# Global keys between the blocks of K^T, a tile of its own for the normalised P, and given steps for the weight conversion

## The chip, the cores and the metric

The kernel runs on one core of a Trainium2 chip. The metric is the device time of one execution in microseconds (us), as the median of several executions. The profile that is read here is of one such execution.

## What is computed

Windowed attention with a few global tokens, and behind it two feed-forward networks, all in fp32:

```
q_l, k_l, v_l: 4 batches x 8 heads x 512 local tokens x 64;   q_g, k_g, v_g: 4 x 8 x 32 global tokens x 64
out_g = softmax(q_g @ [k_g, k_l]^T / 8) @ [v_g, v_l]
s_ll  = q_l @ k_l^T / 8, masked to |i - j| <= 32
out_l = softmax([q_l @ k_g^T / 8, s_ll]) @ [v_g, v_l]
x = concat(out_g, out_l) as 2176 tokens x 512
h = x @ w_in   (512 x 2048);  x = (h * cos(h)) @ w_out   (2048 x 512)
h = x @ w2_in  (512 x 2048);  out = max(h, 0)^2 @ w2_out
```

The weights arrive as float64. The kernel reads them as pairs of 32-bit words and makes an fp32 number of each pair (the conversion), and then splits every fp32 weight and activation into a high and a low part for products in TensorE's fp32r form.

## The kernel before

**Attention.** There are 16 pairs of heads (4 batches x 4). A pair gives two local items of 256 query tokens each, and two pairs share one global item, so that an order of five items repeats eight times: local, local, local, local, global; 40 items in all. One step of the main loop (`for s in range(...)`) takes one item each through several stages, at fixed lags: item s has its scores made on TensorE (PE), item s gets its softmax on VectorE (DVE) and ScalarE (ACT), item s-1 is normalised on GpSimd (POOL) and DVE, item s-2 has its probabilities transposed on PE, item s-3 has those transposes copied out by ACT, item s-4 is multiplied by V. The order of the stages within a step is the list `CFG["order"]`, and every engine works through its own instructions in that order: nothing overtakes.

The names that the rows use: `tk` and `tq` are PE's transposes of K and Q in PSUM, `kT` and `qT` their copies in SBUF; `s` the local scores and `sg` the global ones; `pt` the local probabilities, `pg` their normalised part for the global keys; `st` row sums and their reciprocals; `tw`, `tg` transposes of probabilities and `tws`, `tgs` their copies (`twg`, `tlg`, `ptg`, `tls` for the global item); `o` the output of an item, `xt` its place in the networks' input. `kn`, `qn`, `va`, `vb`, `qgn`, `ktn`, `vgz` are loads.

**K^T.** `kT` of a pair holds 8 rows of 160 columns: 64 keys, the next 64 keys, 32 global keys, so that the scores of one 64-token query block read one row. ACT writes the first 64 columns of each row (`k_evac`, line 336); POOL copies the next row's first 64 columns beside them (line 351), repeats the global keys in all rows (line 353) and puts the tail of the sequence into the last row (line 361). The normalising step (`norm`, lines 468 and 475) works in place in `pt`: one of four units on DVE, three on POOL.

**The conversion of weights.** `Feed` takes jobs (weight block g, half q) one by one. `begin` starts a job when its credit has reached 1 and issues its load `raw` on SyncE's queue (SP, lines 126 and 131); two calls later POOL and ACT make `cu` and `cc` (lines 143 and 146), one call later DVE combines them (lines 154 and 155), and one call later POOL adds them into the ring tile `r` (line 165). In attention `begin` is called once a step and gets 0.5 of credit from step 5 on, except in the steps whose number modulo 5 is 0 or 2 while pairs are left; in the networks it gets 0.5 in every step. `split` makes `w` of a finished block: ACT writes the high parts (line 228, twice), and at the next call of `split` POOL and DVE subtract them (line 214). In attention it is called in the steps of `CFG["split"]`.

The items' number modulo 5 also says what else a step holds: K^T of a later pair in steps 2 and 4 (modulo 5), Q^T in steps 0 and 3, loads of Q and copies of V in step 1, of V in step 3, of K in step 0.

**PSUM and queues.** The transposes `tk`, `tq`, `tw`, `twg` take turns in two banks, `s` and `sg` in three. All loads but Q's first are issued by SP, in program order, on eight semaphores in turn: a load waits for the landing of the one eight places before it.

**Networks.** 160 steps of 24 matmuls each (`g1` into `h`, `g2` into `y`), on the blocks of weights that `split` left; their first four steps are interleaved with attention's last.

Of the kernel before, what the change touches and what calls it, by code (L numbers as in the profile page):

```python
# [10 lines left out]
F32 = mybir.dt.float32  # L11
# [3 lines left out]
AF = mybir.ActivationFunctionType  # L15
ALU = mybir.AluOpType
# [3 lines left out]
P = 128  # L20
NEG = -8.0e9
# [4 lines left out]
CFG = {'order': ['CV', 'LQ', 'S', 'TE', 'BG', 'LK', 'OM', 'TRK', 'KEV', 'CC', 'SM',  # L26
           'RC', 'NM', 'CB', 'LV', 'OE', 'TRQ', 'QE', 'KC', 'TM'],
 'lag': {'S': 0,
         'TRK': -3,
         'TRQ': -2,  # L30
         'KEV': -3,
         'KC': -3,
         'QE': -2,
         'SM': 0,
# [9 lines left out]
         'CV': 11},  # L44
 'ndv': 1,
 'teg': 'AA',
 'free': -5,
 'kb': 'P',
 'split': [22, 24, 27, 29, 33],
 'sx': [32, 34, 37, 39],  # L50
 'arate': 0.5,
 'rate': 0.5,
 's0': 5,
 'groups': [[4, 5, 7], [8, 8]],
 'xd': [0, 1, 2, 3],
 'nr': 6,
 'oe': 'DD',
 'sgb': 0}
GROUPS = CFG["groups"]
RATE, ARATE, XD, NRING = CFG["rate"], CFG["arate"], CFG["xd"], CFG["nr"]  # L60

@with_exitstack
def kernel(
# [14 lines left out]
    nc = tc.nc  # L78
    B, H, SL, D = q_l.shape
    SG = q_g.shape[2]  # L80
# [26 lines left out]
    ident = cpool.tile([P, P], F32, name="ident")  # L107
# [123 lines left out]
    feed = Feed()  # L231
# [21 lines left out]
    lp = late.enter_context(tc.tile_pool(name="lp", bufs=1, side="right"))  # L253
    ep = early.enter_context(tc.tile_pool(name="ep", bufs=1))

    KTB = 2 * 64 + SG
    masks = [ep.tile([P, 160], F32, name=f"mask{i}") for i in range(3)]
    VA = [lp.tile([P, 5, 4, D], F32, name=f"va{i}") for i in range(2)]
    VB = [lp.tile([P, 4, 4, D], F32, name=f"vb{i}") for i in range(2)]
# [2 lines left out]
    ktail = ep.tile([P, NPAIR, B, 64], F32, name="ktail")  # L262
# [3 lines left out]
    kn, qn, kT, qT, tks = {}, {}, {}, {}, {}  # L266
# [54 lines left out]
    def tr_k(p):  # L321
        b, kk = divmod(p, NPAIR)
        tk = bank(BT, "tk")
        for c in range(4):
            nc.tensor.transpose(  # L325
                tk[:, c * P : (c + 1) * P],
                kn[p // 2][:, c, 2 * (p % 2) : 2 * (p % 2) + 2].rearrange("p h d -> p (h d)"),
                ident,
            )
        t = ep.tile([P, 8, KTB], F32, tag="kT", name="kT", bufs=3)  # L330
        kT[p] = t
        tks[p] = tk

    def k_evac(p):
        t, tk = kT[p], tks.pop(p)
        nc.scalar.activation(
            t[:, :, 0:64], tk.rearrange("p (j q) -> p j q", q=64), AF.Copy
        )
        if CFG["kb"] == "A":
            nc.scalar.activation(  # L340
                t[:, :, 128:KTB], tk[:, 0:SG].unsqueeze(1).to_broadcast([P, 8, SG]), AF.Copy
            )
        elif CFG["kb"] == "D":
            nc.vector.tensor_copy(
                t[:, :, 128:KTB], tk[:, 0:SG].unsqueeze(1).to_broadcast([P, 8, SG])
            )

    def k_copy(p):
        t = kT[p]
        one = dict(scalar1=1.0, scalar2=1.0, op0=ALU.mult, op1=ALU.mult)  # L350
        nc.gpsimd.tensor_scalar(t[:, 0:7, 64:128], t[:, 1:8, 0:64], **one)
        if CFG["kb"] == "P":
            nc.gpsimd.tensor_scalar(
                t[:, :, 128:KTB], t[:, 0, 0:SG].unsqueeze(1).to_broadcast([P, 8, SG]), **one
            )
        if p > 1:
            k_tail(p)

    def k_tail(p):
        b, kk = divmod(p, NPAIR)  # L360
        nc.gpsimd.tensor_scalar(
            kT[p][:, 7, 64:128], ktail[:, kk, b, :], 1.0, 1.0, op0=ALU.mult, op1=ALU.mult
        )

    def tr_q(p):
# [37 lines left out]
        load_small(qgn, q_g[b], b)  # L403

    class Local:
# [4 lines left out]
        def s_mm(self):  # L413
            self.s = [bank(BS, "s") for h in range(2)]
            for i in range(2):
                for half in range(2):
                    j = 4 * self.hb + 2 * i + half
                    for h in range(2):
                        d = slice(64 * h, 64 * h + 64)
                        nc.tensor.matmul(  # L420
                            self.s[h][64 * half : 64 * half + 64, 160 * i : 160 * i + 160],
                            lhsT=qT[self.p][d, 64 * j : 64 * j + 64],
                            rhs=kT[self.p][d, j, :],
                            start=True,
                            stop=True,
                            skip_group_check=True,
                        )

        def softmax(self):
            self.pt = lp.tile([P, 4, KTB], F32, tag="pt", name="pt", bufs=4)  # L430
            self.st = lp.tile([P, 3, 4], F32, tag="st", name="st", bufs=4)

            def unit(u):
                i = 2 * self.hb + u % 2
                m = masks[1] if i == 0 else masks[2] if i == 3 else masks[0]
                nc.vector.tensor_tensor_reduce(  # L436
                    out=self.pt[:, u, :],
                    in0=self.s[u // 2][:, 160 * (u % 2) : 160 * (u % 2) + 160],
                    in1=m,
                    scale=-0.125,  # L440
                    scalar=3.0e38,
                    op0=ALU.add,
                    op1=ALU.min,
                    accum_out=self.st[:, 0, u : u + 1],
                )
                nc.scalar.activation(  # L446
                    self.pt[:, u, :],
                    self.pt[:, u, :],
                    AF.Exp,
                    bias=self.st[:, 0, u : u + 1],  # L450
                    scale=-1.0,
                    accum_out=self.st[:, 1, u : u + 1],
                )

            return [lambda u=u: unit(u) for u in range(4)]
# [10 lines left out]
        def norm(self):  # L466
            self.pg = lp.tile([P, 4, SG], F32, tag="pg", name="pg", bufs=2)
            nc.gpsimd.tensor_tensor(
                self.pg,
                self.pt[:, :, P:KTB],  # L470
                self.st[:, 2, :].unsqueeze(2).to_broadcast([P, 4, SG]),
                op=ALU.mult,
            )
            for u in range(4):
                (nc.vector if u < CFG["ndv"] else nc.gpsimd).tensor_scalar(
                    self.pt[:, u, 0:P],
                    self.pt[:, u, 0:P],
                    self.st[:, 2, u : u + 1],
                    1.0,
                    op0=ALU.mult,  # L480
                    op1=ALU.mult,
                )

        def t_mm(self):
            self.tw = bank(BT, "tw").rearrange("p (u q) -> p u q", u=4)
            self.tg = bank(BG, "tg")[:, 0:P]
            for u in range(4):
                nc.tensor.transpose(self.tw[:, u, :], self.pt[:, u, 0:P], ident)  # L488
            nc.tensor.transpose(self.tg, self.pg.rearrange("p u q -> p (u q)"), ident)

        def t_evac(self):
# [42 lines left out]
    class Global:  # L534
# [3 lines left out]
        def s_mm(self):  # L538
            self.s = []
            for n in (320, 256):  # L540
                s = bank(BT if CFG["sgb"] >> (n == 256) & 1 else BS, "sg")
                self.s.append(s)
                for i in range(2):
                    kk = 2 * self.g + i
                    t = kT[self.b * NPAIR + kk]
                    nc.tensor.matmul(  # L546
                        s[64 * i : 64 * i + 64, 0:n],
                        lhsT=qgbd[:, kk, self.b, :],
                        rhs=t[:, 0:5, 0:64] if n == 320 else t[:, 5:8:2, 0:128],
                        start=True,  # L550
                        stop=True,
                    )
# [96 lines left out]
    for h in range(2):  # L649
        s = slice(64 * h, 64 * h + 64)  # L650
        nc.gpsimd.affine_select(
            out=masks[0][s, 0:64], in_=masks[0][s, 0:64], pattern=[[1, 64]],
            compare_op=ALU.is_ge, fill=NEG, base=0, channel_multiplier=-1,
        )
        nc.gpsimd.affine_select(
            out=masks[0][s, 64:128], in_=masks[0][s, 64:128], pattern=[[-1, 64]],
            compare_op=ALU.is_ge, fill=NEG, base=0, channel_multiplier=1,
        )
    for i in (1, 2):
        nc.vector.tensor_copy(masks[i], masks[0])  # L660
    nc.vector.memset(masks[1][0:64, 0:32], NEG)
    nc.vector.memset(masks[2][64:128, 96:128], NEG)
    nc.vector.memset(qgbd, 0.0)

    nc.gpsimd.memset(ktail, 0.0)
# [7 lines left out]
    for b in range(B):  # L673
        for g in range(2):
            for i in range(2):
                p = b * NPAIR + 2 * g + i
# [227 lines left out]
    for s in range(L["TRK"], NI + L["OE"]):  # L904
        due = lambda k: due_tr.get(s - k)
        cb, qe = [], []
        for c in CFG["order"]:
            if c == "BG":
                cb = feed.begin(ARATE if due(CFG["free"]) is None else 0.0) if s >= CFG["s0"] else []
            elif c == "CB":  # L910
                for op in cb:
                    op()
# [111 lines left out]
```

## Time and profile before

| | us |
|---|---|
| median of 3 runs | 911.26 (911.12 to 912.29) |
| the profiled execution's own time | 911.74 |
| its span (first to last instruction) | 910.0 |
| PE busy | 890.7 (98%) |
| DVE, ACT, POOL busy | 502.5, 439.4, 447.8 |

PE's busy time is a sum over instructions whose ends are modelled, so that 98% does not say that PE is at its peak. Attention takes the first 146 us, the networks the rest.

### The profile page before, as it was taken

How to read it: one execution, taken by the hardware profiler on the slowest of the kernel's cores; microseconds unless marked ns; L12 is line 12 of the kernel's file. 1: busy time of each engine (PE TensorE's matmuls, PEld its weight loads, DVE VectorE, ACT ScalarE, POOL GpSimd, SP SyncE). 2: the span in 40 equal slices, each digit the busy share in tenths (PEclk: the TensorE clock that was granted, in tenths of full speed). 3: DMA queues.
4: the chain of work that ended last, by engine and by line, in shares of the span. 5: the costliest groups of instructions: out<-in, count | busy, mean ns of one | idle time of the engine just before them, and what ended most of it. 6: DMA issues, size and time to landing. Idle time of an engine off the chain costs nothing.

```text
span 910.0 us, 15436 instructions
## 1 busy us (share of the span) xinstructions
PE 890.7 (98%) x5720; PEld 793.7 (87%) x5720; DVE 502.5 (55%) x1058; ACT 439.4 (48%) x1036; POOL 447.8 (49%) x517
## 2 busy tenths in 40 slices
PE   7899999999999999999999999999999999999997
PEld 5777777999999999999999988889999888899996
DVE  5687899866776666765554483433422833232221
ACT  5778787665655545545444553333334632222211
POOL 4577888754574435744342484444423842222221
PEclk9999999999999999999999999999999999999999
DMA  7888643221122111121110021111100101010001
GB/s 168 192 192 195 165 129 94 71 70 53 49 62 70 47 53 61 50 70 47 47 47 1 1 70 47 53 44 66 47 1 1 47 1 47 1 47 1 35 35 36
DMA packets 82075, 57.10 MB, mean 63 GB/s; under 512 B 58320, under 2 KB 74704, under 8 KB 82000
## 3 DMA queue, kind: packets, MB, share of 16 engines
q1 hardware_dynamic: 79824, 55.59, 22.0%
q8 instruction: 45, 0.74, 0.3%
q10 hardware_dynamic: 2176, 0.52, 0.3%
q14 instruction: 30, 0.25, 0.1%
HBM read 47.45 MB, written 4.46 MB: 57 GB/s over the span
## 4 chain that ended last, share of the span: by engine, by line
PE 91%; DVE 3%; DMA 2%; ACT 1%; SPq 1%; POOL 1%; issue 1%; ACTq 0%; POOLq 0%; DVEq 0%
PE h L757 41%; PE y L786 41%; PE s L420 2%; PE tw L488 1%; PE o L504 1%; PE tq L368 1%; DVE pt L436 1%; PE o L516 1%; PE og L622 1%; DMA raw<-in_moe_w_out_dram 1%; PE sg L546 1%; PE tk L325 0%; ACT pt L446 0%; SPq L292 0%; PE twg L603 0%
## 5 line engine op out<-in xcount | busy, mean ns | idle before, releaser
L757 PE MATMUL h<-x,w 128*128 128x436 f32 (+3 forms) x1920 | 403.4, 358 | 0.0
L857 POOL TENSOR_TENSOR glo<-cr,ghi 128x436 fp32r<-128x436 f32 (+3 forms) x160 | 186.8, 1167 | 407.7 <-ACT ghi L851 393.9
L757 PEld LDWEIGHTS h<-x,w 128*128 128x128 f32 x1920 | 354.6, 188 | 27.5
L786 PE MATMUL y<-ghi,w 128*128 128x436 f32 (+1 forms) x640 | 177.6, 358 | 0.0
L846 DVE TENSOR_TENSOR cr<-h,cr 128x436 f32<-128x436 f32 (+3 forms) x160 | 96.6, 605 | 134.0 <-ACT cr L837 115.0
L786 PE MATMUL y<-w,ghi 128*128 128x512 f32 x544 | 168.4, 390 | 0.0
L745 DVE TENSOR_TENSOR x<-xt,x 128x436 fp32r<-128x436 f32 (+3 forms) x100 | 102.5, 1035 | 93.3 <-ACT x L744 78.3
L837 ACT ACTIVATE cr<-h 128x384 f32<-128x384 f32 (+1 forms) x80 | 42.8, 535 | 210.7 <-PE h L757 209.4
L786 PEld LDWEIGHTS y<-ghi,w 128*128 128x128 f32 x640 | 120.3, 188 | 6.1
L786 PEld LDWEIGHTS y<-w,ghi 128*128 128x128 f32 x544 | 101.4, 188 | 18.9
L786 PE MATMUL y<-glo,w 128*128 128x436 f32 (+1 forms) x320 | 114.8, 359 | 0.0
L786 PE MATMUL y<-w,glo 128*128 128x512 f32 x272 | 106.8, 393 | 0.0
L851 ACT ACTIVATE ghi<-cr 128x436 fp32r<-128x436 f32 (+3 forms) x160 | 89.7, 560 | 24.5 <-DVE cr L846 23.6
L831 ACT ACTIVATE ck<-h 128x436 int32<-128x436 f32 (+1 forms) x80 | 42.6, 532 | 113.1 <-PE h L757 113.1
L833 DVE SCALAR_TENSOR_TENSOR cr<-h,ck 128x436 f32<-128x436 f32 (+1 forms) x80 | 48.6, 607 | 84.9 <-ACT ck L831 84.9
L165 POOL TENSOR_TENSOR r<-cu,cc 128x512 uint32<-128x512 uint32 x64 | 85.0, 1328 | 2.0 <-DVE cc L155 2.0
L744 ACT ACTIVATE x<-xt 128x436 fp32r<-128x436 f32 (+3 forms) x100 | 55.1, 560 | 20.2 <-PE h L757 19.9
L786 PEld LDWEIGHTS y<-glo,w 128*128 128x128 f32 x320 | 60.1, 188 | 2.7
L786 PEld LDWEIGHTS y<-w,glo 128*128 128x128 f32 x272 | 51.0, 188 | 10.8
L842 ACT ACTIVATE cr<-cr,halfpi 128x436 f32<-128x436 f32 (+1 forms) x80 | 52.5, 657 | 10.1 <-DVE cr L833 10.1
L155 DVE SCALAR_TENSOR_TENSOR cc<-raw,cc 128x512 uint32<-128x512 uint32 x64 | 55.7, 870 | 0.0
L446 ACT ACTIVATE pt<-pt,st 128x160 f32<-128x160 f32 x128 | 53.3, 425 | 4.1 <-DVE st L436 4.1
(91 smaller groups left out, 907.4 us busy)
## 6 DMA issues: line engine op xcount, KB each, us to landing
raw<-in_moe_w_in_dram SPq DMA_DIRECT2D x32, 512.0 KB, 3.7
raw<-in_moe_w_out_dram SPq DMA_DIRECT2D x32, 512.0 KB, 3.5
vb<-va SPq DMA_DIRECT2D x16, 256.0 KB, 4.6
out_dram<-ypart SPq DMA_DIRECT2D x16, 256.0 KB, 2.1
qn<-in_q_l_dram SPq DMA_DIRECT2D x28, 128.0 KB, 3.7
va<-in_v_l_dram SPq DMA_DIRECT2D x24, 128.0 KB, 3.3
kn<-in_k_l_dram SPq DMA_DIRECT2D x21, 128.0 KB, 3.0
va<-in_v_l_dram SPq DMA_DIRECT2D x8, 96.0 KB, 3.2
```

The costliest lines, as they stand in the source:

```text
L155: lambda: v.scalar_tensor_tensor(c, t[:, :, 1].bitcast(U32), 0x80000000, c, op0=ALU.bitwise_and, op1=ALU.bitwise_or,),
L165: nc.gpsimd.tensor_tensor(ring[g][:, q, :].bitcast(U32), u, c, op=ALU.add)
L446: nc.scalar.activation(self.pt[:, u, :], self.pt[:, u, :], AF.Exp, bias=self.st[:, 0, u : u + 1], scale=-1.0, accum_out=self.st[:, 1, u : ...
L744: nc.scalar.activation(hi, xr, AF.Copy)
L745: return lambda: (nc.vector if kk in XD else nc.gpsimd).tensor_tensor(lo, xr, hi.bitcast(F32), op=ALU.subtract)
L757: nc.tensor.matmul(h, lhsT=w[:, ws, 0, kk * P : (kk + 1) * P], rhs=x, start=(k == 0), stop=(k == 3 * NK - 1),)
L786: nc.tensor.matmul(o, lhsT=l, rhs=r, start=(c_first and k == 0), stop=(c_last and k == 2))
L833: lambda: nc.vector.scalar_tensor_tensor(r, h, INV2PI, k, op0=ALU.mult, op1=ALU.subtract),
L842: nc.scalar.activation(ctmp[s], ctmp[s], AF.Sin, bias=halfpi, scale=TWOPI)
L846: nc.vector.tensor_tensor(r, hps.pop(s), r, op=ALU.mult)
L851: nc.scalar.activation(ghi[s], ctmp[s], AF.Copy)
L857: nc.gpsimd.tensor_tensor(lo, ctmp.pop(s), hi.bitcast(F32), op=ALU.subtract)
```

## The change

Four things. (1) `kT` has 9 rows of 96 columns: 64 keys and the 32 global keys behind them. The scores of block j read 160 columns from 96j on, which are block j, the global keys and block j+1. So line 351 is gone, and the masks and slices follow the new order of columns. (2) `norm` writes the normalised local part into a tile `pn` (2 buffers) instead of into `pt`, whose buffers go from 4 to 3. (3) Conversion in attention begins in 13 listed steps, and `split` is called in other steps. (4) In the networks the credit is 0.55 a step. Only the last two move instructions between steps.

```diff
- 'free': -5,
- 'split': [22, 24, 27, 29, 33],
+ 'split': [21, 26, 31, 36, 39],
- 'arate': 0.5,
- 'rate': 0.5,
- 's0': 5,
+ 'begin': [9, 11, 14, 16, 19, 21, 24, 26, 29, 31, 34, 36, 39],
+ 'rate': 0.55,
...
+    GK = slice(64, 64 + SG)
...
-        t = ep.tile([P, 8, KTB], F32, tag="kT", name="kT", bufs=3)
+        t = ep.tile([P, 9, 64 + SG], F32, tag="kT", name="kT", bufs=3)
...
     def k_copy(p):
-        nc.gpsimd.tensor_scalar(t[:, 0:7, 64:128], t[:, 1:8, 0:64], **one)
-        if CFG["kb"] == "P":
-            nc.gpsimd.tensor_scalar(
-                t[:, :, 128:KTB], t[:, 0, 0:SG].unsqueeze(1).to_broadcast([P, 8, SG]), **one
-            )
+        nc.gpsimd.tensor_scalar(
+            t[:, 0:8, GK], t[:, 0, 0:SG].unsqueeze(1).to_broadcast([P, 8, SG]), **one
+        )
...
+    def windows(t, u):
+        return t.rearrange("p u q -> p (u q)")[:, KTB * u : KTB * u + 192].rearrange(
+            "p (a q) -> p a q", a=2
+        )[:, :, 0:64]
...
-                            rhs=kT[self.p][d, j, :],
+                            rhs=kT[self.p].rearrange("p j q -> p (j q)")[d, 96 * j : 96 * j + KTB],
...
-            self.pt = lp.tile([P, 4, KTB], F32, tag="pt", name="pt", bufs=4)
+            self.pt = lp.tile([P, 5, KTB], F32, tag="pt", name="pt", bufs=3)
...
-                self.pt[:, :, P:KTB],
+                self.pt[:, 0:4, GK],
...
+            self.pn = lp.tile([P, 4, P], F32, tag="pn", name="pn", bufs=2)
             for u in range(4):
                 (nc.vector if u < CFG["ndv"] else nc.gpsimd).tensor_scalar(
-                    self.pt[:, u, 0:P],
-                    self.pt[:, u, 0:P],
+                    self.pn[:, u].rearrange("p (a q) -> p a q", a=2),
+                    windows(self.pt, u),
...
-                nc.tensor.transpose(self.tw[:, u, :], self.pt[:, u, 0:P], ident)
+                nc.tensor.transpose(self.tw[:, u, :], self.pn[:, u], ident)
...
-                cb = feed.begin(ARATE if due(CFG["free"]) is None else 0.0) if s >= CFG["s0"] else []
+                cb = feed.begin(1.0 if s in CFG["begin"] else 0.0)
```

The changed kernel's lines stand two to five lower in number: its 124, 129, 141, 144, 163, 212, 226 are before's 126, 131, 143, 146, 165, 214, 228, and its 342, 463, 471 are 353, 468, 475.

On SP's queue, around step 16 (the load of Q in `qn`), before:

```order
L309 DMA vb_88<-va_86 64x1024
L310 DMA vb_88<-va_86 64x1024
L292 DMA qn<-in_q_l_dram 128x4x64 x4
L397 DMA qgn<-in_q_g_dram 32x8x64
L131 DMA raw<-in_moe_w_out_dram 128x1024
L299 DMA va_85<-in_v_g_dram 32x4x64
```

and changed:

```order
L308 DMA vb_88<-va_86 64x1024
L309 DMA vb_88<-va_86 64x1024
L291 DMA qn<-in_q_l_dram 128x4x64 x4
L129 DMA raw<-in_moe_w_out_dram 128x1024
L386 DMA qgn<-in_q_g_dram 32x8x64
L298 DMA va_85<-in_v_g_dram 32x4x64
```

The weight load of step 18 is now that of step 16, and its two readers stand in step 18 instead of step 20.

On POOL, from the end of step 15 to step 18, before (`ptg` closes step 15, `cu` opens step 16, and the K^T copies close step 17):

```order
L595 TENSOR_SCALAR ptg<-ptg,stg 128x544
L143 TENSOR_SCALAR cu<-raw 128x512
L468 TENSOR_TENSOR pg<-pt,st 128x128
L475 TENSOR_SCALAR pt<-pt,st 128x128 x3
L468 TENSOR_TENSOR pg<-pt,st 128x128
L475 TENSOR_SCALAR pt<-pt,st 128x128 x3
L351 TENSOR_SCALAR kT<-kT 128x7x64
L353 TENSOR_SCALAR kT<-kT 128x8x32
L361 TENSOR_SCALAR kT<-ktail 128x64
L165 TENSOR_TENSOR r<-cu,cc 128x512
L468 TENSOR_TENSOR pg<-pt,st 128x128
L475 TENSOR_SCALAR pt<-pt,st 128x128 x3
```

and changed:

```order
L591 TENSOR_SCALAR ptg<-ptg,stg 128x544
L141 TENSOR_SCALAR cu<-raw 128x512
L463 TENSOR_TENSOR pg<-pt,st 128x128
L471 TENSOR_SCALAR pn<-pt,st 128x128 x3
L463 TENSOR_TENSOR pg<-pt,st 128x128
L471 TENSOR_SCALAR pn<-pt,st 128x128 x3
L342 TENSOR_SCALAR kT<-kT 128x8x32
L350 TENSOR_SCALAR kT<-ktail 128x64
L141 TENSOR_SCALAR cu<-raw 128x512
L163 TENSOR_TENSOR r<-cu,cc 128x512
L463 TENSOR_TENSOR pg<-pt,st 128x128
L471 TENSOR_SCALAR pn<-pt,st 128x128 x3
```

The big copy of K^T is gone, and step 18 has a `cu`, which waits for a weight load, ahead of its `r` and its normalising.

On ACT, steps 21 to 23, before (`tws<-twg` belongs to step 22, the `kT` behind it too):

```order
L446 ACTIVATE pt,st<-pt,st 128x160 x4
L611 ACTIVATE tws<-twg 128x512
L612 ACTIVATE tls<-tlg 32x128
L336 ACTIVATE kT<-tk 128x8x64
L446 ACTIVATE pt,st<-pt,st 128x160 x4
L228 ACTIVATE w<-r 128x512 x2
L494 ACTIVATE tws<-tw 128x512
```

and changed:

```order
L441 ACTIVATE pt,st<-pt,st 128x160 x4
L226 ACTIVATE w<-r 128x512 x2
L607 ACTIVATE tws<-twg 128x512
L608 ACTIVATE tls<-tlg 32x128
L335 ACTIVATE kT<-tk 128x8x64
L441 ACTIVATE pt,st<-pt,st 128x160 x4
L490 ACTIVATE tws<-tw 128x512
```

The two writes of `w` have gone from the end of step 22 to the end of step 21.

## Rows read from the trace of the kernel before

**Rows 1.** The page's first part: busy us (share) xinstructions.

```profile
PE 890.7 (98%) x5720; PEld 793.7 (87%) x5720; DVE 502.5 (55%) x1058; ACT 439.4 (48%) x1036; POOL 447.8 (49%) x517
```

**Rows 2.** Stretches: length, busy us of PE, PEld, DVE, ACT, POOL, clock, DMA.

```profile
50.00:100.00 50.00, 47.49 (x730) 38.06 (x726) 41.07 (x188) 39.57 (x148) 38.93 (x78) 0.97 0.82 187
100.00:150.00 50.00, 46.93 (x717) 36.85 (x716) 43.67 (x173) 39.97 (x146) 42.68 (x77) 1.00 0.47 125
200.00:250.00 50.00, 50.00 (x257) 48.03 (x256) 33.51 (x49) 29.73 (x58) 25.92 (x23) 1.00 0.18 55
```

**Rows 3.** Line 351's instructions: duration ns min/median/max, first and last start us.

```profile
L351 POOL TENSOR_SCALAR kT<-kT x16: 556/561/986, 6.5 to 130.4; 128x448 f32<-128x448 f32 x16
```

**Rows 4.** PE in order of time: start, us, operation [idle before <-releaser].

```profile
99.64 0.66 PE L603 MATMUL twg<-ident,ptg 128*128 128x128 f32 x4 [0.45 <-POOL ptg L595]
109.74 1.03 PE L488 MATMUL tw<-ident,pt 128*128 128x128 f32 x3 [0.25 <-POOL pt L475]
```

**Rows 5.** POOL in order of time, ahead of the first of these.

```profile
96.39 1.26 POOL L214 TENSOR_TENSOR w<-r,w 128x512 fp32r<-128x512 f32 x1
```

**Rows 6.** Step 23 on ACT and PE, in order of time.

```profile
85.81 1.14 ACT L228 ACTIVATE w<-r 128x512 fp32r<-128x512 f32 x2
87.49 0.98 PE L368 MATMUL tq<-ident,qn 128*128 128x128 f32 x4 [0.61 <-ACT tws L494]
```

**Rows 7.** The stretch behind it; the clock stands after the busy times.

```profile
86.00:92.00 6.00, 5.39 (x58) 4.05 (x57) 4.00 (x17) 4.45 (x15) 3.65 (x10) 0.72 0.57 128
```

**Rows 8.** DVE and PE around steps 33 to 35, in order of time.

```profile
124.81 0.68 DVE L214 TENSOR_TENSOR w<-r,w 128x512 fp32r<-128x512 f32 x1
...
128.20 0.77 PE L420 MATMUL s<-kT,qT 64*64 64x160 f32 x14 [1.30 <-ACT ptg L571]
```

**Rows 9.** PE in the first steps of the networks.

```profile
151.00 0.28 PE L606 MATMUL tlg<-ident,ptg 128*32 128x128 f32 x1 [0.68 <-ACT tgs L498]
```

**Rows 10.** A blocked DVE instruction: line 460's durations in ns.

```profile
L460 DVE TENSOR_SCALAR st<-st x32: 159/166/1245, 14.3 to 142.7; 128x4 f32<-128x4 f32 x32
```

**Rows 11.** POOL beside it.

```profile
139.77 1.28 POOL L165 TENSOR_TENSOR r<-cu,cc 128x512 uint32<-128x512 uint32 x1
```

**Rows 12.** Steps 13 and 14 on ACT, POOL and PE, in order of time.

```profile
55.92 0.69 ACT L146 ACTIVATE cc<-raw 128x512 uint32<-128x512 uint32 x1 [2.17 <-DMA raw<-in_moe_w_out_dram]
...
55.97 0.68 POOL L143 TENSOR_SCALAR cu<-raw 128x512 f32<-128x512 f32 x1 [1.18 <-PE sg L546]
56.62 0.40 POOL L468 TENSOR_TENSOR pg<-pt,st 128x128 f32<-128x128 f32 x1
57.00 1.07 POOL L475 TENSOR_SCALAR pt<-pt,st 128x128 f32<-128x128 f32 x3
...
58.80 0.66 PE L488 MATMUL tw<-ident,pt 128*128 128x128 f32 x4 [0.98 <-ACT tws L494]
```

**Rows 13.** SP's queue, steps 16 to 18, in order of time.

```profile
65.94 3.09 SPq L292 DMA_DIRECT2D qn<-in_q_l_dram  x4
69.08 0.50 SPq L397 DMA_DIRECT2D qgn<-in_q_g_dram  x1
69.75 0.35 SPq L131 DMA_DIRECT2D raw<-in_moe_w_out_dram  x1
```

**Rows 14.** DMA issues up to 160 us: KB each, median us to landing.

```profile
raw<-in_moe_w_out_dram SPq DMA_DIRECT2D x7, 512.0 KB, 4.3
```

**Rows 15.** Step 18 on ACT and POOL, step 19 on PE, in order of time.

```profile
70.72 0.26 ACT L498 ACTIVATE tgs<-tg 128x128 f32<-128x128 f32 x1
70.88 0.43 ACT L446 ACTIVATE pt<-pt,st 128x160 f32<-128x160 f32 x1
...
72.95 1.09 POOL L475 TENSOR_SCALAR pt<-pt,st 128x128 f32<-128x128 f32 x3
...
74.53 0.60 PE L488 MATMUL tw<-ident,pt 128*128 128x128 f32 x4
```

More of the change, by code (lines that the diff above doesn't have):

```diff
@@ L59 @@
 GROUPS = CFG["groups"]
-RATE, ARATE, XD, NRING = CFG["rate"], CFG["arate"], CFG["xd"], CFG["nr"]
+RATE, XD, NRING = CFG["rate"], CFG["xd"], CFG["nr"]
 @with_exitstack
@@ L336, in k_evac @@
         nc.scalar.activation(
-            t[:, :, 0:64], tk.rearrange("p (j q) -> p j q", q=64), AF.Copy
+            t[:, 0:8, 0:64], tk.rearrange("p (j q) -> p j q", q=64), AF.Copy
         )
-        if CFG["kb"] == "A":
-            nc.scalar.activation(
-                t[:, :, 128:KTB], tk[:, 0:SG].unsqueeze(1).to_broadcast([P, 8, SG]), AF.Copy
-            )
[L343 to L346, printed above, removed]
     def k_copy(p):
@@ L350, in k_copy @@
         one = dict(scalar1=1.0, scalar2=1.0, op0=ALU.mult, op1=ALU.mult)
-        nc.gpsimd.tensor_scalar(t[:, 0:7, 64:128], t[:, 1:8, 0:64], **one)
-        if CFG["kb"] == "P":
-            nc.gpsimd.tensor_scalar(
-                t[:, :, 128:KTB], t[:, 0, 0:SG].unsqueeze(1).to_broadcast([P, 8, SG]), **one
-            )
+        nc.gpsimd.tensor_scalar(
+            t[:, 0:8, GK], t[:, 0, 0:SG].unsqueeze(1).to_broadcast([P, 8, SG]), **one
+        )
         if p > 1:
@@ L361, in k_tail @@
         nc.gpsimd.tensor_scalar(
-            kT[p][:, 7, 64:128], ktail[:, kk, b, :], 1.0, 1.0, op0=ALU.mult, op1=ALU.mult
+            kT[p][:, 8, 0:64], ktail[:, kk, b, :], 1.0, 1.0, op0=ALU.mult, op1=ALU.mult
         )
@@ L548, in s_mm @@
                         lhsT=qgbd[:, kk, self.b, :],
-                        rhs=t[:, 0:5, 0:64] if n == 320 else t[:, 5:8:2, 0:128],
+                        rhs=t[:, 0:5, 0:64] if n == 320 else t[:, 5:9, 0:64],
                         start=True,
@@ L655 @@
         nc.gpsimd.affine_select(
-            out=masks[0][s, 64:128], in_=masks[0][s, 64:128], pattern=[[-1, 64]],
+            out=masks[0][s, 96:160], in_=masks[0][s, 96:160], pattern=[[-1, 64]],
             compare_op=ALU.is_ge, fill=NEG, base=0, channel_multiplier=1,
@@ L661 @@
     nc.vector.memset(masks[1][0:64, 0:32], NEG)
-    nc.vector.memset(masks[2][64:128, 96:128], NEG)
+    nc.vector.memset(masks[2][64:128, 128:160], NEG)
     nc.vector.memset(qgbd, 0.0)
```

## The prediction

> **What bounds the kernel now.** I read the busy times first: PE is busy for 890.7 of 910.0 us [rows 1], so at most some 19 us can be won by removing waits of PE. Then the stretches, to see where those lie: from 200 us on PE is busy for 50.00 of 50.00 us, while between 50 and 150 us it lacks 2.51 and 3.07 us per 50 [rows 2]. The reader is to see that the networks are bound by PE alone and only attention has something to give, and that there the other engines have no room to spare: DVE 41 to 44, ACT 40, POOL 39 to 43 of 50 us [rows 2]. Then PE's instructions in order of time, for what ended each of its waits. I found no single limit but single places where another engine comes late: POOL in steps 26 and 29 [rows 4], ACT in step 23 [rows 6], ACT behind DVE in step 35 [rows 8], ACT in the networks' first steps [rows 9], and a weight load in steps 13 and 14 [rows 12]. The faster credit in the networks and the smaller tiles touch nothing on which PE waits: with DVE at 33.51 and POOL at 25.92 of 50 us beside a full PE [rows 2], 0.55 instead of 0.5 jobs a step is hidden. I cost both at nothing; the cover is PE's own work.
>
> **The parts of the change, one by one.** The sum is made against the profiled execution, 911.74 us; its span is 910.0 and 1.74 lie around it. The median of the three runs, 911.26, is 0.48 lower, and I take that off at the end.
>
> *(a) K^T without the big copy.* 16 instructions of 0.561 us, 9.0 us, leave POOL [rows 3]. No PE instruction waits for them alone, as POOL has time between the steps. Against that, conversion is denser: by the lists, 12 instead of 10 `cu` and 11 instead of 9 `r` stand before step 40, which at 0.68 and 1.28 us [rows 11, 12] gives 3.9 us back to POOL. Where POOL is late, it counts. In step 26 PE waits 0.45 us for POOL's `ptg` [rows 4]. Ahead of that stood, in POOL's order, a K^T copy (0.56) and a `w` of 1.26 us [rows 5], which the new `split` steps put behind step 26's normalising. That is 1.8 us sooner, and the 0.45 goes; next late is PE itself. In step 29 the normalised units come one by one: 0.25 us of wait and three transposes in 1.03 us, where four in a row take 0.60 [rows 4, 15], so 0.68 us; there too a `w` and a copy move ahead. Together I take 1.1 us; bounds 0 (POOL is late again because of the denser `cu`, or the copies were hidden anyway) and 1.8 (with all 16 copies' cover counted in the steps between).
>
> *(b) ACT's `w` from step 22 to step 21.* In step 23 PE waits 0.61 us for a bank that `tws` empties, and on ACT just ahead of that stand two `w` of together 1.14 us [rows 6]. Moved a step up they fall before a `kT` for which ACT has to wait on PE anyway, so the 0.61 goes. Right behind this wait the granted clock of PE falls: over the 6 us from 86 on its mean is 0.72, which is a stretch at the lower level, 1.2 instead of 2.4 GHz, and a loss of 0.28 x 6 = 1.7 us [rows 7]. Whether that stays away I can't tell from one trace: the wait of 0.98 us in step 14 [rows 12] had no fall behind it, since the whole loss of the stretch from 50 to 100 us (0.03 x 50 = 1.5) is that one [rows 2, 7]. So I take 0.6 and half of 1.7, 1.45 us; bounds 0.6 and 2.3.
>
> *(c) DVE's `w` from step 33 to step 36.* It takes 0.68 us just ahead of the global softmax for whose end PE waits 1.30 us in step 35 [rows 8]. A conversion's DVE part moves from step 31 to step 32, where DVE waits for ACT in part. I take 0.6; bounds 0 and 1.3.
>
> *(d) The first steps of the networks.* Three instead of four conversions end in steps 40 to 43. PE waits 0.68 us there, behind ACT [rows 9]. I take 0.3; bounds 0 and 0.7.
>
> *(e) POOL and DVE hold each other up.* A DVE instruction on 4 elements takes 0.166 us as a rule and up to 1.245 [rows 10], and such a one lies beside a POOL instruction of 1.28 us [rows 11]. Fewer POOL instructions hold DVE less often. I take 0.5 us of gain; from the same rows it can be a loss (below). In the new tile `pn` the instructions have the shapes they had in place, so I cost it at nothing; its two buffers are written two items later, when PE has long read them. If the strided reading of `pt` cost 0.05 us, that would be 1.6 us of DVE and 4.8 of POOL over all, spread beside PE.
>
> *(f) The weight loads.* The change adds a wait. In step 13 before, ACT waits 2.17 us for a weight load and POOL's `cu` as well; PE lost 0.98 us by it [rows 12]. That load stays where it was (step 11), but now an `r` stands between `cu` and the normalising: POOL's units end 1.28 later than 58.07, and the last of PE's four transposes, which began at 58.80 [rows 12], comes some 0.3 us later. The same happens anew in step 18, whose load is issued in step 16, behind four loads of Q. SP has those out at 69.03 in the trace, and only then could the load start [rows 13]; it needs 0.35 and 4.3 us to landing [rows 13, 14], so it is there at 73.7. ACT is ready for it at 70.88 [rows 15] and would wait 2.8 us with all its exponentials behind it. POOL then does `cu` 0.68, `r` 1.28, `pg` 0.40 and three units in 1.07 us and ends at 77.1; before, it ended at 74.04, and PE's four transposes start at 74.53 and are wanted to their end at about 75.0 [rows 12, 15]. That is 2.1 us late, less the 0.3 by which PE is behind already: 1.8, and I take 1.9 for what ACT adds. Bounds: 0 (SP runs ahead and the load lands by 71) and 4.6 (ACT's 2.8 in full, and a clock fall of 1.7 behind it).
>
> The sum: 1.1 + 1.45 + 0.6 + 0.3 + 0.5 = 3.95 of gains, 0.3 + 1.9 = 2.2 of losses, 1.75 net. 911.74 - 1.75 = 909.99; less 0.48 this is **909.5 us**.
>
> **The rivals.**
>
> *The load in step 18 decides, and it gets slower.* The place is `cu` on POOL and `cc` on ACT in step 18; from a landing later than about 71.5 us on, POOL ends after PE wants the units, and each us more is one of PE's. With a PE that stands for 2 us the clock may fall as it did behind step 23, 1.7 us [rows 7]. Then 2.2 + 1.7 of losses stand against (a) and (c) alone, 1.7, since what (b) saves is lost here: 911.74 + 2.2 - 0.48 = 913.5. For it: the load in step 13 shows the same wait, and SP's order leaves no way around. Against it: waits of PE up to 1.30 us [rows 8] passed without a fall.
> The Trainium skill ("TensorE: Matmul & The Clock Gate", HAM oscillation — how this bites in real kernels) says that gaps in PE's work, such as waits for loads, bring it back to the lower clock. The trace agrees for step 23 (0.72) and not for step 14 (1.00 but for that one stretch).
>
> *Nothing is won: added POOL instructions hold DVE.* Two more `r` before step 40, each able to hold a small DVE instruction for 1.245 - 0.166 = 1.1 us [rows 10, 11], take 2.2 us from DVE, which is at 43.67 of 50 [rows 2]. Then (e) is a loss of 1.7 instead of a gain of 0.5, and the sum is 909.5 + 2.2 = 911.7. Against it: the held ones are mostly off PE's path, as POOL's normalising, not DVE's, is what PE waits for [rows 4].
> The Trainium skill ("SBUF — State Buffer", Who interferes with whom) states such a lock: POOL and a DVE instruction that uses both ports, or two SBUF inputs, block each other for a whole instruction. Rows 10 and 11 agree, 1.245 against 0.166 us.
>
> *The load is no trouble and all waits go.* If SP is earlier in step 16, since loads up to there differ in place, (f) is 0; with the upper bounds of (a) 1.8 and (b) 2.3, half of those of (c) and (d), 1.0, and (e) 0.5, the gain is 5.6: 911.74 - 5.6 - 0.48 = 905.7. For it: split and conversion now keep apart from the steps with K^T and Q^T, so that several places relax at once. Against it: rows 13.
>
> **How the numbers follow.** The forecast has 0.42, its own range 907.5 to 911.5; the slower rival 0.21, the one without gain 0.10, the fast one 0.27. No change means within 0.2% (1.8 us), about what can be measured. The forecast lies at that edge, so half of it counts as faster: 0.20 + 0.27 = 0.47 faster; 0.20 + 0.10 = 0.30 the same; 0.21 and 0.02 of the forecast's upper end 0.23 slower. The range reaches to both outer rivals and a little past the fast one, 904.0 to 913.5. On the slow side that is less than the sums of all bounds on the median's scale, 911.26 - 6.6 = 904.7 with every gain and no loss, and 911.26 + 4.6 + 1.7 + 0.3 - 0.6 = 917.3 with every loss, which don't fall together.
>
> **What the changed profile would show.** For (a): PE's `twg` in step 26 without a wait for `ptg`. For (b): `tq` in step 23 without a wait, and a clock of 1.00 from 80 to 100 us. For (c): a wait under 1 us in step 35. For (f): ACT's `cc` in step 18 waiting some 2.8 us for `raw`, and a wait of PE for `pn` some 2 us long in step 19. The prediction is wrong if that wait isn't there (then 906 or less), if the clock falls behind it, or if time goes in the networks, where I expect PE at 50.00 of 50 us from 200 us on.

## The result, and the profile after

The changed kernel is slower: 922.31 us median (918.31 to 923.04, 4 runs) against 911.77 for the kernel before (911.12 to 913.22, 4 runs), ratio 1.0102, 95% interval [1.0074, 1.0130]. 909.5 was forecast, and the range ended at 913.5.

The profiled execution is the fastest of the four, 918.31 us with a span of 916.4. The first part of its page, busy us (share) xinstructions, and the three stretches that answer to [rows 2], with the clock behind the busy times:

```profile
PE 894.6 (98%) x5720; PEld 794.6 (87%) x5720; DVE 514.5 (56%) x1058; ACT 440.4 (48%) x1036; POOL 442.2 (48%) x501
```

```profile
50.00:100.00 50.00, 46.80 (x708) 37.33 (x710) 42.06 (x181) 38.05 (x142) 36.76 (x71) 0.97 0.89 192
100.00:150.00 50.00, 44.57 (x694) 34.03 (x688) 44.76 (x174) 40.61 (x148) 40.47 (x70) 1.00 0.50 132
200.00:250.00 50.00, 50.00 (x255) 47.59 (x255) 32.49 (x50) 29.55 (x57) 25.81 (x24) 1.00 0.18 60
```

PE's busy time grew less than the span; what it lacks in attention grew from 2.51 and 3.07 us per 50 [rows 2] to 3.20 and 5.43. The list of waits up to 170 us (who waited for what: sum of us, times, longest) names the new waits, of ACT for a weight load and of PE for the copy that ACT then makes late:

```profile
ACT cc L144 <- DMA raw<-in_moe_w_out_dram: 8.3, 4, 3.5
...
PE tw L484 <- ACT tws L490: 4.2, 2, 2.3
```

Before, these two were 2.17 and 0.98 us, once each [rows 12]. The four waits for loads on ACT, in order of time (start, us, operation, idle before); they stand in steps 13, 18, 23 and 28:

```profile
56.99 0.67 ACT L144 ACTIVATE cc<-raw 128x512 uint32<-128x512 uint32 x1 [3.49 <-DMA raw<-in_moe_w_out_dram]
...
74.12 0.69 ACT L144 ACTIVATE cc<-raw 128x512 uint32<-128x512 uint32 x1 [0.56 <-DMA raw<-in_moe_w_out_dram]
...
90.43 0.69 ACT L144 ACTIVATE cc<-raw 128x512 uint32<-128x512 uint32 x1 [1.24 <-DMA raw<-in_moe_w_out_dram]
...
110.17 0.68 ACT L144 ACTIVATE cc<-raw 128x512 uint32<-128x512 uint32 x1 [3.06 <-DMA raw<-in_moe_w_out_dram]
```

Where these loads come from is seen on SP's queue, here in step 26, and in the issues from 100 to 112 us (KB each, us to landing):

```profile
100.41 0.47 SPq L308 DMA_DIRECT2D vb<-va  x1
101.14 0.47 SPq L309 DMA_DIRECT2D vb<-va  x1
101.72 2.88 SPq L291 DMA_DIRECT2D qn<-in_q_l_dram  x4
104.77 0.38 SPq L129 DMA_DIRECT2D raw<-in_moe_w_out_dram  x1
```

```profile
raw<-in_moe_w_out_dram SPq DMA_DIRECT2D x1, 512.0 KB, 5.3
```

Two copies of V and four loads of Q go ahead of it. 104.77 + 5.3 = 110.07, and ACT starts at 110.17. On PE the waits come one step later, in steps 14 and 29 (the row between them, of step 27, has nothing to do with a load; it belongs to (b)):

```profile
59.85 0.87 PE L484 MATMUL tw<-ident,pn 128*128 128x128 f32 x4 [2.27 <-ACT tws L490]
...
104.27 0.66 PE L484 MATMUL tw<-ident,pn 128*128 128x128 f32 x4 [0.66 <-ACT tws L607]
...
113.03 0.89 PE L484 MATMUL tw<-ident,pn 128*128 128x128 f32 x4 [1.91 <-ACT tws L490]
```

Behind the first of them the clock falls, as the first of these two stretches shows (0.72):

```profile
61.00:67.00 6.00, 6.00 (x83) 5.00 (x83) 4.97 (x20) 3.19 (x14) 4.59 (x8) 0.72 0.96 167
86.00:92.00 6.00, 5.87 (x86) 4.50 (x86) 5.09 (x21) 4.76 (x19) 4.23 (x8) 1.00 0.56 146
```

The second answers to [rows 7]: the fall of before is gone there, and so is the wait of [rows 6] (`tq` starts at 89.75 with no wait ahead). But a second trace of the unaltered kernel before (below) has the wait without the fall. So that trace, span 908.0 and clock 1.00, is the cleaner one to compare with. A step is counted from PE's first score product to that of the next, step 39 to the networks' first product into `h`; the steps that aren't listed differ by less than 0.2 each and cancel out; us:

| step | before, second trace | after | difference |
|---|---|---|---|
| 14 and 15 | 7.69 | 10.51 | +2.82 |
| 22 | 2.88 | 3.24 | +0.36 |
| 23 | 4.51 | 3.84 | -0.67 |
| 26 and 27 | 6.23 | 7.33 | +1.10 |
| 29 | 4.09 | 5.51 | +1.42 |
| 30, 33 and 34 | 10.26 | 11.31 | +1.05 |
| 35 | 4.66 | 3.61 | -1.05 |
| 36 to 39 | 14.95 | 16.99 | +2.04 |
| networks | | | +1.3 |

These sum to 8.4, the difference of the spans.

### The profile page after: what moved, and what is told of

It is laid out like the page before. It is cut to its first block, busy times and chain, and to the rows that moved or that the text cites. A ratio compares the mean times of both kernels' runs of the same rounds, so it can differ in the third digit from the quotient of the medians.

```text
span 916.4 us, 15431 instructions
## 1 busy us (share of the span) xinstructions
PE 894.6 (98%) x5720; PEld 794.6 (87%) x5720; DVE 514.5 (56%) x1058; ACT 440.4 (48%) x1036; POOL 442.2 (48%) x501
## 4 chain that ended last, share of the span: by engine, by line
PE 89%; DVE 4%; DMA 2%; ACT 1%; SPq 1%; issue 1%; POOL 0%; ACTq 0%; POOLq 0%; DVEq 0%
PE h L753 41%; PE y L782 41%; PE s L415 2%; DMA raw<-in_moe_w_out_dram 1%; DVE pt L431 1%; PE tw L484 1%; PE o L500 1%; PE og L618 1%; SPq L291 1%; PE o L512 1%; ACT pt L441 1%; PE tq L357 1%; DVE st L455 1%; PE sg L542 1%; PE tk L324 0%
## 5 line engine op out<-in xcount | busy, mean ns | idle before, releaser
L153 DVE SCALAR_TENSOR_TENSOR cc<-raw,cc 128x512 uint32<-128x512 uint32 x64 | 62.2, 972 | 0.0
L152 DVE TENSOR_SCALAR cu<-cu 128x512 uint32<-128x512 uint32 x64 | 53.4, 835 | 12.1 <-POOL cu L141 12.0
```

Of the source, the lines that this page charges most:

```text
L152: lambda: v.tensor_scalar(u, u, 3, None, op0=ALU.logical_shift_left),
L153: lambda: v.scalar_tensor_tensor(c, t[:, :, 1].bitcast(U32), 0x80000000, c, op0=ALU.bitwise_and, op1=ALU.bitwise_or,),
```

## The experiments

The expectations speak of four theories: L, the weight loads land late because of their place in SP's queue; D, conversion is too dense; P, the new tiles cost by their strides; N, the networks' faster credit. All ratios are to the kernel before, run beside it on the same chip (its median is in the third column), with 95% intervals.

| kernel | median us (range, runs) | before beside it | ratio |
|---|---|---|---|
| layout_only | 914.37 (913.00 to 915.81, 10) | 912.62 | 1.0019 [1.0004, 1.0033] |
| tables_only | 921.70 (920.22 to 923.04, 4) | 912.62 | 1.0098 [1.0079, 1.0118] |
| credit_050 | 920.77 (920.32 to 922.18, 4) | 912.62 | 1.0096 [1.0080, 1.0111] |
| load_a_step_ahead | 913.68 (912.25 to 914.71, 10) | 912.62 | 1.0012 [0.9999, 1.0024] |
| raw_first | 917.80 (915.34 to 921.61, 6) | 912.24 | 1.0065 [1.0044, 1.0086] |
| begin_of_before | 913.76 (912.24 to 917.41, 12) | 912.24 | 1.0023 [1.0010, 1.0036] |
| split_only | 911.78 (910.78 to 913.71, 11) | 912.24 | 0.9993 [0.9984, 1.0002] |
| before_split_ahead | 910.87 (909.09 to 912.50, 12) | 912.24 | 0.9986 [0.9975, 0.9997] |
| split_at_37 | 910.37 (908.65 to 912.11, 12) | 912.14 | 0.9985 [0.9972, 0.9998] |
| split_mixed | 909.80 (908.60 to 911.36, 12) | 912.14 | 0.9981 [0.9968, 0.9994] |
| ahead_split_37 | 913.87 (911.32 to 916.52, 12) | 912.14 | 1.0025 [1.0009, 1.0040] |
| before_credit_055 | 911.53 (910.74 to 914.30, 10) | 911.79 | 0.9999 [0.9979, 1.0019] |

**Layout or tables: layout_only, tables_only, credit_050.** The change in halves, and the whole with 0.5 in place of 0.55.

```diff
 layout_only (in the changed kernel)
- 'split': [21, 26, 31, 36, 39], 'begin': [9, 11, 14, ...], 'rate': 0.55,
+ 'free': -5, 'split': [22, 24, 27, 29, 33], 'arate': 0.5, 'rate': 0.5, 's0': 5,
...
 tables_only (in the kernel before): the same lines the other way
 credit_050 (in the changed kernel)
- 'rate': 0.55,
+ 'rate': 0.5,
```

> The new K^T layout and the tile pn, with the steps of conversion and split and the credit of the kernel before. Theory L (the weight loads that begin in steps 11, 16, 21 and 26, behind the copies of V and the loads of Q, make ACT and POOL wait): the loads stand where they stood, so ACT waits once, some 2.2 us in step 13, and the time is that of before or up to 2 us less, 909.5 to 912. Theory D (density of the conversion): the same. Theory P (reading pt with a stride and writing pn costs DVE and POOL): 915 or more.

> The layout and the in-place normalising of before, with the new steps of conversion and split and the new credit. Theory L: ACT waits for loads as in the changed kernel, some 8 us in all, and the time is that of the changed kernel, 918 to 923. Theory D: the same or 1 to 3 us above it, since POOL has the big copies as well. Theory P: the time of before, 911 to 913.

> The changed kernel with a credit of 0.5 instead of 0.55 in the networks. Theories L, D and P: nothing, 920 to 923, since PE is busy throughout in the networks. A rival, theory N (the denser conversion in the networks costs): 2 to 5 us less.

The tables alone cost nearly the whole loss (9.1 us), and the credit gives next to nothing back: P and N fall as its main cause. The layout alone costs 1.8 us, which no theory had as it stood (L and D: the time of before or less; P: 915 or more). In the trace of tables_only the load of step 11 makes ACT wait 4.72 us, and PE 3.48:

```profile
60.77 0.66 ACT L147 ACTIVATE cc<-raw 128x512 uint32<-128x512 uint32 x1 [4.72 <-DMA raw<-in_moe_w_out_dram]
...
63.60 1.12 PE L489 MATMUL tw<-ident,pt 128*128 128x128 f32 x4 [3.48 <-ACT tws L495]
```

Ahead of the networks credit_050 is the changed kernel itself, so that its trace is one more look at the same attention. There the load of step 16 is waited for too, on ACT in step 18 and on PE in step 19:

```profile
75.09 0.69 ACT L144 ACTIVATE cc<-raw 128x512 uint32<-128x512 uint32 x1 [3.19 <-DMA raw<-in_moe_w_out_dram]
...
77.95 0.88 PE L484 MATMUL tw<-ident,pn 128*128 128x128 f32 x4 [2.33 <-ACT tws L490]
```

ACT's waits for weight loads are 1.9, 2.9, 3.2 and 3.6 us here, for the loads of steps 9, 11, 16 and 26, 11.6 in sum where the first trace of after has 8.7 (the 8.3 above and 0.3 for the load of step 9). Step 19 takes 5.93 us instead of 3.32, and the execution takes 920.42 us.

**The loads sooner: load_a_step_ahead, raw_first.** The first keeps every conversion where the change put it and only issues its load one step earlier; the second issues it in its own step, but ahead of V's copies and Q's loads.

```diff
+        def ahead(self):
+            if self.jobs and self.jobs[0][0] < self.nsplit + NR and self.jobs[0] not in raw:
+                conv_load(*self.jobs[0])
...
 load_a_step_ahead: behind begin
+                if s + 1 in CFG["begin"]:
+                    feed.ahead()
 raw_first: at the step's start
+        if s in CFG["begin"]:
+            feed.ahead()
```

> The changed kernel, with each of the 13 listed weight loads issued one step earlier; cu, cc, r, w stay in their steps, so density and order on POOL, DVE and ACT are untouched. Theory L: the waits of ACT for the load go from 8.3 us to under 1, and the time falls by 4 to 8 us, to 911 to 916. Theory D and theory P: no more than 2 us of change, 918 to 922.

> The changed kernel, but in each listed step the weight load is issued first, ahead of the step's two copies of V and four loads of Q, in the same step as before. Theory L (the load's place in SP's queue behind these six transfers makes it late): ACT's waits for raw fall from 8.3 us to under 2, and the time to 914 to 916. Rival T (what helped a step ahead was the extra step of time, since issue to landing takes 4.4 to 4.9 us in any case): the load lands hardly sooner, ACT still waits 5 us or more in sum, and the time stays at 919 to 922.

A step ahead, no wait of ACT for a weight load is left, and 8 to 9 us of the loss go. On SP the load of step 26 now stands ahead of K's loads of step 25:

```profile
93.76 0.35 SPq L129 DMA_DIRECT2D raw<-in_moe_w_out_dram  x1
...
100.58 0.59 SPq L314 DMA_DIRECT2D vb<-va  x1
101.27 3.03 SPq L296 DMA_DIRECT2D qn<-in_q_l_dram  x4
```

With the same conversions in the same steps, D falls too: density costs nothing that can be seen once the loads are there. The raw_first kernel missed its number: 914 to 916 expected, 917.8 measured (rival T had 919 to 922). ACT's wait in step 13 is gone and steps 14 and 29 take 3.15 and 3.16 us instead of 5.85 and 5.51, as L has it. But as step 19 now comes 2.9 us sooner, the load of step 19, which SP issues behind six loads of V in both kernels and which landed in time only because the changed kernel was late, is late itself; and the clock falls behind the wait that follows. ACT and PE in order of time, and the stretch behind:

```profile
81.06 0.68 ACT L144 ACTIVATE cc<-raw 128x512 uint32<-128x512 uint32 x1 [1.79 <-DMA raw<-in_moe_w_in_dram]
...
84.97 0.66 PE L489 MATMUL tw<-ident,pn 128*128 128x128 f32 x4 [1.65 <-ACT tws L612]
```

```profile
85.00:91.00 6.00, 6.00 (x70) 5.08 (x71) 3.02 (x16) 5.15 (x21) 4.96 (x11) 0.57 0.84 142
```

**Steps apart: begin_of_before, split_only, before_credit_055.**

```diff
 begin_of_before (in the changed kernel)
- 'begin': [9, 11, 14, 16, 19, 21, 24, 26, 29, 31, 34, 36, 39],
+ 'begin': [8, 11, 14, 18, 21, 24, 28, 31, 34, 36, 38],
 split_only (in the kernel before)
- 'split': [22, 24, 27, 29, 33],
+ 'split': [21, 26, 31, 36, 39],
 before_credit_055 (in the kernel before)
- 'rate': 0.5,
+ 'rate': 0.55,
```

> The changed kernel with its new layout, split list and credit, but conversion begins in the steps in which it began before (8, 11, 14, 18, 21, 24, 28, 31, 34, 36, 38). Theory L: the two loads of steps 16 and 26 behind Q's loads are gone, those of 11, 21 and 31 stay as they were before; ACT's waits for raw are 2 to 3 us, and the time is 913 to 915. Rival S (the split steps or the number of conversions carry the loss): 917 or more.

> The kernel before with the changed split list alone (21, 26, 31, 36, 39). Prediction's parts (b) and (c): PE's wait of 0.61 in step 23, the half-clock stretch behind it and part of the wait of 1.30 in step 35 go, 2.3 to 3 us, so 909.5 to 910.5 where the kernel before has 912.5. Rival (the saving is taken back by a clock fall elsewhere, or the networks run 1.3 us longer as in every altered kernel so far): 911 to 913.

> The kernel before with 0.55 in place of 0.5 conversions a step in the networks, nothing else. The prediction cost this part at nothing: within 0.5 us of the kernel before. If the density of conversion sets the networks' pace, steps 4 to 15 take 4.75 us each and the time is 1.3 us longer; if the steps ahead of step 40 do, they take 4.64.

With before's begin steps the changed kernel is within 0.23% of the one before, so the begin list carries most of the loss. Up to step 13 the only difference between the two begin lists is 9 in place of 8, and that is enough to make the load of step 11 later: ACT waits 2.9 to 4.7 us for it in the four traces with a load in step 9 (after, after_again, credit_050, tables_only), and 2.2 us at most in the six with one in step 8. The credit alone changes nothing. The split list alone, on which (b) and (c) rested, gives 0.5 us of 2.3 to 3 expected, not to be told from nothing. Its trace shows that the waits only moved: against before's second trace, steps 23, 29 and 35 are 0.7, 0.9 and 1.1 us shorter, and steps 27, 30 and 38 are 0.9, 0.7 and 1.1 longer. The networks are 1.4 us longer besides, which its rival had named. Step 27, ACT and PE in order of time:

```profile
99.22 1.14 ACT L228 ACTIVATE w<-r 128x512 fp32r<-128x512 f32 x2
100.26 0.57 ACT L611 ACTIVATE tws<-twg 128x512 f32<-128x512 f32 x1
...
100.89 0.66 PE L488 MATMUL tw<-ident,pt 128*128 128x128 f32 x4 [0.66 <-ACT tws L611]
```

It is the picture of [rows 6] again: two `w` of ACT just ahead of a copy that PE wants.

**What comes and goes: before_again, after_again.** Both kernels unaltered, one more trace of each.

> The kernel before once more, unaltered, for a second trace of it. If the pace of the networks' steps 4 to 15 (4.64 us a step in the first trace of before, 4.75 in that of every altered kernel) belongs to the kernel, it is 4.64 here; if it differs from execution to execution, it may be 4.75 here. The same for the half-clock stretch behind step 23 at 87.7 us: if the wait of 0.61 us brings it, it is here again; if it comes and goes, it is elsewhere or gone.

> The changed kernel once more, unaltered, for a second trace. Theory L: ACT waits again for the weight loads of steps 11, 16, 21 or 26, 9 us or more in sum in an execution of 921 to 923 us, against 8.3 us in the one of 918.3. Rival: the waits for loads are the same 8 us, and what more a usual execution takes lies in half-clock stretches alone.

In the second trace of before PE waits in step 23 as in [rows 6], and the clock stays up. PE's row, and the stretch that answers to [rows 7]:

```profile
87.20 0.66 PE L368 MATMUL tq<-ident,qn 128*128 128x128 f32 x4 [0.59 <-ACT tws L494]
```

```profile
86.00:92.00 6.00, 5.38 (x70) 4.13 (x66) 5.41 (x22) 5.12 (x18) 4.55 (x11) 1.00 0.67 168
```

The second trace of after took 918.15 us with a wait of 3.41 us for the load of step 11 on ACT and one of 2.19 on PE; step 14 and the clock fall behind it are as in the first, the wait of 1.91 in step 29 is 0.67, and a fall near 33 us is new. ACT's waits for loads sum to 6.1 us, so that neither side of its expectation was met: it wasn't an execution of 921 us. What a slower one has more is seen in the trace of credit_050 above: waits for loads, 11.6 us of them.

**POOL's w in step 38, and the best version: before_split_ahead, split_at_37, split_mixed, ahead_split_37.** In the changed kernel step 38 shows how (c) was given back. DVE, POOL and ACT in order of start:

```profile
138.49 0.68 DVE L212 TENSOR_TENSOR w<-r,w 128x512 fp32r<-128x512 f32 x1
...
140.07 1.30 DVE L455 TENSOR_SCALAR st<-st 128x4 f32<-128x4 f32 x1
...
140.08 1.26 POOL L212 TENSOR_TENSOR w<-r,w 128x512 fp32r<-128x512 f32 x1
...
144.29 0.43 ACT L441 ACTIVATE pt<-pt,st 128x160 f32<-128x160 f32 x1 [1.40 <-DVE st L431]
```

The DVE instruction works on 4 elements and takes 0.166 us by its median [rows 10]; beside POOL's `w` it takes 1.30, all that DVE does next is late by that, and the next item's exponentials wait 1.40 us for DVE. The Trainium skill ("SBUF — State Buffer", Who interferes with whom) states that POOL and a DVE instruction that uses both ports block each other for a whole instruction; the two rows agree.

```diff
 before_split_ahead (split_only, with the load of the coming begin issued a step ahead)
+                if s + 1 >= CFG["s0"] and due(CFG["free"] - 1) is None and feed.credit + ARATE >= 1.0:
+                    feed.ahead()
...
 split_at_37 (the same) and ahead_split_37 (load_a_step_ahead)
- 'split': [21, 26, 31, 36, 39],
+ 'split': [21, 26, 31, 37, 39],
 split_mixed (the same)
+ 'split': [21, 24, 27, 29, 37, 39],
```

> The kernel before with the changed split list, and each weight load of attention issued one step ahead. Theory L: ACT's wait of 2.17 us in step 13 goes too, and PE's 0.98 behind it; 908.5 to 910. Rival (a load issued earlier pushes K's and Q's loads back, and PE then waits 1 to 2.5 us for these, in step 6 above all): 911 to 913, no better than the split list alone.

> As before_split_ahead, with split step 36 put at 37. Theory H (POOL's w of 1.26 us in step 38 holds DVE's instruction on 4 elements for 1.30 instead of 0.17 us, and the exponentials of step 39 wait 1.4 us for it): step 38 takes 3.0 us as it did before instead of 4.1, and the time falls by 0.5 to 1.1 us, to 909.8 to 910.4 where the kernel before has 912.2. Rival (another POOL instruction falls on that DVE instruction, or DVE's own w of 0.68 us makes the step late): step 38 stays at 3.8 us or more, no change.

> As before_split_ahead, with the split steps 21, 24, 27, 29, 37 and 39: the first from the changed list, the next three from the list before. With ACT's w at 26 and 31, steps 27 and 30 each take 0.7 to 0.9 us longer than before; with it at 24 and 29 these go. Theory: 1 us faster than split_at_37, 909 to 909.5. Rival (before lost 0.8 us in step 24 and 0.9 in step 29 by the same w, so it is a trade): within 0.3 us of split_at_37.

> The changed kernel with each weight load a step ahead and split step 36 at 37. Theory H: step 38 is 1.1 us shorter than in load_a_step_ahead, 912.6 to 913.2 in place of 913.7, so that the changed kernel is level with the one before. Rival: as for split_at_37, 913.7.

With 37 in place of 36, DVE and POOL in step 38 in order of start:

```profile
138.24 0.52 DVE L465 TENSOR_SCALAR st<-st 128x4 f32<-128x4 f32 x1
```

```profile
134.88 2.62 POOL L480 TENSOR_SCALAR pt<-pt,st 128x128 f32<-128x128 f32 x3
137.47 1.27 POOL L219 TENSOR_TENSOR w<-r,w 128x512 fp32r<-128x512 f32 x1
```

The DVE instruction now meets only the end of POOL's `w`, and step 38 takes 3.45 us instead of 4.14 in before_split_ahead, steps 36 to 39 together 15.8 instead of 16.4. So the mechanism holds, with 0.6 us where 1.1 was expected; in the medians (910.87 and 910.37, 913.68 and 913.87) it can't be told from nothing. The first of these kernels, before_split_ahead itself, came out between its theory (908.5 to 910) and its rival (911 to 913), and its trace has something of both: no wait of ACT for a weight load is left, but PE waits 1.5 and 0.6 us for Q's loads in step 3. The mixed list has the lowest median, 0.19% below the kernel before. Its expectation of a further 1 us isn't settled by the medians (910.37 and 909.80, intervals overlap); by the trace it is the trade that the rival named: against split_at_37, steps 27 and 30 win 0.9 and 0.7 us, and steps 26 and 29 lose 0.6 and 0.9. The trace has an attention with a clock of 1.00, and from 50 us to the end of step 38 no wait of PE over 0.57 us:

```profile
0.00:150.00 150.00, 139.63 (x2000) 109.45 (x2002) 119.30 (x512) 114.92 (x418) 109.82 (x224) 1.00 0.74 169
```

In step 39 there is a new one, for normalising that POOL does just behind the `w` that went to step 37, a `cu` and an `r`:

```profile
138.44 0.68 PE L493 MATMUL tw<-ident,pt 128*128 128x128 f32 x2 [1.11 <-POOL pt L480]
```

PE's first score product of step 39 is at 134.98 us, where before's second trace, which has a clock of 1.00 too, has it at 137.75: 2.8 us are won ahead of it. From there on the mixed list is 1.9 us slower, 1.4 of it in the networks, and so 0.9 us are left of the span.

## Why the prediction was wrong

**(f) is the step that failed.** It priced one new load, that of step 16, at 1.9 us, the one of step 11 at 0.3 and that of step 26 not at all. The place that made it late, behind V's copies and Q's loads, is that of steps 11, 16, 21 and 26, where before had 11 and 21 (in steps 31 and 36 no loads of Q are left). The load of step 11, which kept its place, comes later too, since the one ahead of it moved from step 8 to step 9. The mechanism and even the landing were right (73.7 forecast for the load of step 16; ACT's `cc` started at 74.12), but in the profiled execution ACT waited only 0.56 us for it, since step 14 had made everything 2.8 us late; in credit_050's, where steps 14 and 15 lost less, ACT waited 3.19 and PE 2.33 us for it, close to the 2.8 and 1.9 that were forecast. In the profiled execution the first and the last decide: ACT's 3.49 and 3.06 us, PE's 2.27 and 1.91, with the fall behind the first (step 15, +1.3). Steps 14, 15 and 29 lose 4.2 us there where 2.2 stood in the sum; sooner loads won back 8 to 9 us of the median. The prediction's own sign of being wrong pointed the other way: without the wait in step 19 it had 906 or less, and the first trace is without it. (By its own terms, 2.8 and 1.7, the upper bound of (f) is 4.5, not 4.6.)

From 1.8 us of gain to 10.5 of loss are 12.3 us. My estimate from the runs above: 6 to 7 of them are (f), 8 to 9 instead of 2.2; 4 are the gains of (a) to (e), which didn't come; 1.3 are the networks. The rival in which the load decides had the right sign and one place of four: 913.5.

**(a)** 1.1 was forecast. PE's wait for `ptg` in step 26 is gone, as said, but in its place PE waits 0.69 us there for DVE's `qT` (at 99.09; 0.78 in layout_only), which I hadn't looked for; and layout_only is 1.8 us slower than before, not faster. 1.3 us of that is the networks' pace (below), so the copies were hidden: the lower bound, 0. The tile `pn` costs nothing by its rows: POOL's instructions take 0.368 us by the median where they took 0.371.

**(b)** The wait of 0.61 us went, as forecast (step 23, -0.67). The half of the clock fall that I counted with it, 0.85 us, was no property of the kernel before: its second trace has the same wait and no fall. And ACT's next `w`, moved to step 26, makes PE wait 0.66 us in step 27, which I didn't look for. Net nothing.

**(c)** The wait in step 35 went wholly (-1.05 where 0.6 was forecast) and came back in step 38 (+1.09) by POOL's half of the same `w`, which I hadn't followed.

**(d)** The interleaved steps won nothing: PE waits 0.68 us behind ACT's `tgs` as before (now at 156.09), and step 39 is 0.18 us longer.

**(e)** had the wrong sign, 0.5 us of gain forecast: the held instruction of step 38, the same 1.1 us that (c) gave back, is its own mechanism, as the second rival had it, with a `w` in place of an `r`.

**The cover of the networks** held against the credit (before_credit_055: 0.9999), but not against time lost there: PE was busy for 50.00 of 50 us and yet 1.3 us slower. That I read "busy" as "at the same pace" is the second failure.

What stays open: the profiled executions of the changed kernel, 918.31 and 918.15, are 3 to 5 us below its other runs (921.65 to 923.04). Those have granted clocks of 0.992 to 0.994 over the span where the profiled ones have 0.995 and 0.994, which is worth 3 us at most. That loads which land later account for the rest is likely by the trace of credit_050, but those executions themselves left no trace.

## What to carry to other kernels

When a table moves an operation, follow its load to the place in the queue that each of its steps gives it, for all of its steps and not the first, and ask who is ready for it by then; the cheapest repair is to issue it a step sooner and leave its readers alone. A wait that a move takes away has to be looked for at the step it moved to, on every engine that holds a part of the work. A late stage hides the next late transfer: what one repair wins, the next load may take.

## What the hardware showed unexpectedly

The networks' steps 4 to 15 have two paces at a granted clock of 1.00 and without a wait. PE's 12 products of a step in after, and in the second trace of before:

```profile
173.51 2.53 PE L753 MATMUL h<-x,w 128*128 128x436 f32 x12
```

```profile
161.60 2.48 PE L757 MATMUL h<-x,w 128*128 128x436 f32 x12
```

A step takes 4.75 us in one and 4.64 in the other (178.25 - 173.51 is 4.74, 166.24 - 161.60 is 4.64). Both traces of before and before_credit_055 have 4.64, and the twelve kernels whose layout or tables ahead of step 40 differ have 4.75; from step 16 on all are alike. So something ahead of the networks sets it; what, none of the runs tells.

Falls of the clock come and go with executions of one program: at 87.7 us in one trace of before and nowhere in the other, at 20 us in one of after and near 33 in the other. Only the one behind step 14's wait of over 2 us was in both traces of after. The Trainium skill ("TensorE: Matmul & The Clock Gate", HAM oscillation — how this bites in real kernels) has gaps in PE's work bring the lower clock; the gaps of 2.27 and 2.19 us in the two traces of after agree, that of 2.33 in credit_050 doesn't (the clock is 1.00 from 76 to 84 us), and the same gap of 0.6 us in two traces of before has it both ways.
